# Chunk 4's decay factors on another queue, and two weight transfers made four

## The chip, the cores and the metric

The kernel runs on one core of a Trainium2 chip. A core has a matrix engine (TensorE, PE in the profile; its weight loads are the row PEld), a vector engine (VectorE, DVE), a scalar engine (ScalarE, ACT), a general engine (GpSimd, POOL) and an engine that here only issues transfers (SyncE, SP). They run their own instruction streams and wait for each other by semaphores. Transfers are issued from POOL, SP or ACT and carried by 16 DMA engines that all queues share. The metric is the device time of one execution in microseconds (us); lower is better.

## The reference

Two stages follow each other: a gated linear attention, and a bilinear feed-forward layer on its output.

```python
# q, k, v, alpha: (4, 8, 768, 48); alpha between 0.8 and 1.0
for t in range(S):
    state = alpha[:, :, t, :, None] * state + np.einsum('bhd,bhe->bhde', k[:, :, t], v[:, :, t])
    y[:, :, t] = np.einsum('bhd,bhde->bhe', q[:, :, t], state)
x = y.transpose(0, 2, 1, 3).reshape(3072, 384)
out = ((x @ w_a) * (x @ w_b)) @ w_out        # w_a, w_b: (384, 1536), w_out: (1536, 384)
```

## The kernel before

**Tiling.** The work is cut into six chunks. A chunk holds two of the four batches (chunks 0, 2, 4 the first two, 1, 3, 5 the other two) and 256 of the 768 time steps; time goes on from chunk 0 to 2 to 4. Inside a chunk the two batches are called pair 0 and pair 1 (`u`), and the 256 steps lie as 128 partitions by two neighbouring steps (`r`).

**One chunk of attention.** Its alphas are loaded (`ld a`), their logarithm is taken on ScalarE (`ln`, line 420), neighbouring steps are added (`l2`, `lx`), split in a rounded part and a rest (`H`, `L`, or `R` in later chunks) and summed over time on PE (`A2`, `AQ`). ScalarE makes the exponentials (`E`, line 541) and a ratio (`ra`, line 519). POOL or DVE corrects one of the two steps of q and k in place (`lv`, line 526; the k form reads the alphas again). DVE multiplies k and q with the exponentials into the tile QKp (`mk`, `mq`, line 552). QKp is turned so that the head dimension lies on the partitions: in chunks 0 and 1 by PE (`C`, line 593, copied by `Ce`), from chunk 2 on by a transposing transfer on SP (`T`, line 604). Then come the scores (`D`, line 674), their masking (`M`, or `Mc` on ScalarE and `Mm` on DVE), the state update (`K`, `KA`, `k`) and the outputs: `SB` opens the output banks and adds what one half carries into the other, `SA` adds what the carried state gives, `Y` adds the masked scores times v. `X` copies the result out of PSUM; from chunk 2 on it is turned by another transposing transfer on SP (`XT`, line 771).

**The feed-forward layer.** d_ff is cut into twelve blocks of 128 columns. `a f w` and `b f w` multiply block f of w_a or w_b with the chunk's y (line 786); w is `0` or `1` for one pair (256 columns, three matmuls) or `*` for both (512 columns). `as` copies the a product to SBUF on ScalarE (line 792), `pr` multiplies it with the b product on DVE (line 800). `o` multiplies by w_out (line 808), `ot` copies the result and `st` stores it on SP. The last number of a PE step is its PSUM bank, of eight; a step that takes a bank waits until the reader of what stood in it is through.

**Order.** The whole order is written out by hand in the string PROGRAM (lines 17 to 267), one step after the other, as `chunk: step arguments`. Each engine runs its own steps in this order; the letters V, P, S and Y at a step's end choose DVE, POOL, ScalarE or SP. A step that has to wait holds up whatever comes behind it on its engine. A transfer takes one of eight semaphores of its queue in turn, so an issue also waits until the eighth transfer before it on that queue has landed.

**What the change touches.** The weights w_a and w_b come on POOL's queue (`W w lo hi`, line 393), cast from float32 to bfloat16 on the way, in columns 0 to 256, 256 to 768 and 768 to 1536. A feed-forward block f uses columns 128 f to 128 f + 128, so columns 256 to 768 are the blocks 2 to 5. Chunk 0's feed-forward starts on lines 20 to 46 of PROGRAM with pair 0, while pair 1's attention is still under way, and chunk 1's attention is woven into it.

The tiles of the alphas (`a_t`) have two buffers, so chunk 4 takes chunk 2's, after chunk 2's `lv` of k. Chunk 4's alphas are issued on POOL's queue (line 98), between `lv 1 k P` and `lv 0 q P` of chunk 2. Chunk 5's are issued on SP's queue (line 142), just behind chunk 2's two turned outputs (`XT 1`, `XT 0`). The logarithm's tile has one buffer. A gate is one element copied on POOL, which makes POOL wait for what that element belongs to:

```python
def gate_m(x, u, h):
    nc.gpsimd.tensor_copy(go, x.m[int(u), int(h)][0:1, 0, 0, 0, 0:1])
```

Of the kernel before, what the change touches and what calls it, by code (L numbers as in the profile page):

```python
# [20 lines left out]
0: cm 1; ld v 1 P; c2 P; c3 P; D 0 1 5; M 0 1; D 0 0 0; SB 0 6; B 1a 4; Bs 1a; Mc 0 0; Mm 0 0 V; B 1b 5; Bs 1b; E 1a i; E 1a b; mq 1a V; mk 1a V; K 0 1 4; E 1b i  # L21
0: v 1 V; mk 1b V; E 1b b; mq 1b V; SA 0; Y 0; X 0 S; dk 1 0; C 1 0 3; Ce 1 0 V; k 0 1 V; b 1 0 6; W a 0 256; de 1; K 1 0 5; k 1 0 V
1: ld a 1 P
0: W a 256 768; W b 256 768
1: ld a 0 P
0: W a 768 1536; C 1 1 1; a 1 0 2; as 1 0; pr 1 0; Ce 1 1 V; W b 768 1536
1: ld q 0 P; ln 1
0: b 0 0 4; a 0 0 2; as 0 0; pr 0 0; D 1 0 6; D 1 1 0; M 1 1
1: ld k 0 P; l2 1 P; ld v 0 P; ld k 1 P
0: Mc 1 0; Mm 1 0 V  # L30
1: H 1 S
0: SB 1 1; a 2 0 3; a 5 0 6; a 3 0 7; as 3 0; a 4 0 4; as 4 0; as 5 0; b 4 0 0; b 3 0 7
1: L 1 V
0: pr 4 0; pr 3 0; SA 1; Y 1; X 1 V; b 2 0 0
1: A2 1 7; ld q 1 P
0: Wo 0 6
2: ld a * P
0: K 1 1 5
1: ln 0
0: as 2 0; pr 2 0  # L40
1: l2 0 V; E 1 b; E 1 i; H 0 S
0: a 3 1 4; a 5 1 2; k 1 1 V; as 3 1; b 3 1 0; a 4 1 1; b 5 0 7; pr 5 0; as 5 1; a 6 * 5; b 5 1 4; a 11 * 3; pr 5 1; pr 3 1; as 4 1; b 4 1 1; pr 4 1
1: L 0 V; dk * 6
0: Wo 6 12; as 11 *; as 6 *
1: ra 0
0: b 6 * 3; pr 6 *; b 11 * 0; pr 11 *
# [1 line left out]
1: lv 0 q P  # L48
2: ld q * P
1: ld v 1 P; lv 0 k V; mk 0 V  # L50
0: a 10 * 2; a 7 * 3
1: E 0 b; mq 0 V
0: as 10 *; a 2 1 4; as 2 1; b 10 * 1; pr 10 *; as 7 *; b 7 * 0; pr 7 *
1: v 0 S; ra 1
0: b 2 1 3; a 0 1 5
1: C 0 0 4
0: a 1 1 6; as 1 1
1: Ce 0 0 S
0: pr 2 1; b 1 1 1; pr 1 1; as 0 1
1: KA 0 02; k 0 0 V; k 0 1 V; C 0 1 7  # L60
0: b 0 1 6
1: Ce 0 1 S
2: ld k * P
1: lv 1 k P
0: pr 0 1
1: mk 1 V; lv 1 q P; mq 1 V
3: ld a * P
0: a 8 * 1; as 8 *; a 9 * 5; as 9 *
2: ld v * P
0: b 8 * 2; pr 8 *  # L70
1: D 0 0 6; M 0 0; D 0 1 3; Mc 0 1; SB 0 4
# [21 lines left out]
1: a 7 0 3; b 11 0 1; pr 11 0; KA 1 64; k 1 0 V; k 1 1 V; b 10 0 5; a 10 0 7; as 10 0; a 0 0 6  # L93
2: lv 0 k V
1: pr 10 0; b 0 0 1; a 3 0 4; as 0 0; pr 0 0
2: lv 1 k P; mk 1 V
1: as 3 0; b 3 0 7; a 1 0 6; as 1 0
4: ld a * P
1: b 7 0 0; b 1 0 4; pr 1 0; as 7 0; pr 7 0; pr 3 0
2: mk 0 V  # L100
1: SB 1 0
3: ln *
1: a 6 0 2; as 6 0; b 9 0 3; a 4 0 5; a 9 0 6; as 9 0; pr 9 0
2: mq 1 V; T 1
0: o 2 0 4
1: b 4 0 6; b 6 0 7
2: lv 0 q P; mq 0 V
1: pr 6 0
2: T 0
3: ld k * Y  # L110
# [24 lines left out]
2: D 0 0 5; Mc 0 0; Mm 0 0 V; gatem 0 0; SB 0 1; SA 1; Y 1; X 1 S; XT 1  # L135
3: lv 0 k P; lv 1 k P
1: a 4 1 7
4: ln *
1: as 4 1; b 9 1 0; pr 9 1; o 0 0 5
3: AQ 3  # L140
2: SA 0; Y 0; X 0 S; XT 0
5: ld a * Y
1: o 0 1 -; ot 0 V; a 1 1 6; a 10 1 1; as 1 1; as 10 1
3: E 0 b; E 0 i
1: b 4 1 2; pr 4 1; b 8 1 5; b 1 1 1; a 8 1 6; b 10 1 0; pr 1 1; o 3 0 2; pr 10 1; as 8 1; pr 8 1; o 3 1 -; ot 3 S; st 3 Y
# [3 lines left out]
3: E 1 i  # L149
1: st 0 Y  # L150
3: dr
4: lx V; R 0
3: mk 0 V; mq 0 V; T 0
4: ld q * Y
2: a 1 * 2; b 5 * 0; as 5 *; pr 5 *
4: ra 1
2: b 7 * 4; b 10 * 1; pr 4 *; a 10 * 6; as 10 *; pr 10 *
3: mk 1 V
2: a 7 * 0; b 1 * 5; a 0 * 6; b 0 * 7; as 1 *; as 7 *; pr 1 *; pr 7 *; as 0 *; a 3 * 0; b 9 * 1; pr 0 *
3: mq 1 V  # L160
# [5 lines left out]
3: KA * 06; D 0 0 4; M 0 0; dl; k * 0 V; k * 1 V  # L166
1: o 1 0 2
2: b 11 * 7
5: ln *
2: a 11 * 5; as 11 *; pr 11 *  # L170
1: o 1 1 -; ot 1 S
2: a 6 * 5; as 6 *; a 8 * 3; as 8 *
3: SB 0 6; D 0 1 0; M 0 1; T 1
4: ld k * Y
3: D 1 0 4; Mc 1 0
2: b 6 * 2; pr 6 *; b 8 * 3; pr 8 *
4: R 1
# [16 lines left out]
3: a 11 * 5  # L194
2: ot 2 V; ot 3 V
4: mq 0 V; mk 0 V
5: lx V
3: a 9 * 3; a 0 * 2; a 8 * 6; b 11 * 7; as 9 *; as 11 *; as 0 *; pr 11 *; b 9 * 2; b 0 * 1; pr 9 *
5: lv 0 k V
3: as 8 *  # L200
# [70 lines left out]
def kernel(  # L271
# [11 lines left out]
    nc = tc.nc  # L283
    B, H, S, D = q.shape
    assert (B, H, S, D) == (4, 8, 768, 48)
    C = 128
# [14 lines left out]
    ld = ctx.enter_context(tc.tile_pool(name="ld", bufs=2))  # L301
# [21 lines left out]
    go = cst.tile([1, 1], F32, name="go")  # L323
    S0 = [cst.tile([C, B, D + P2 * VS], BF16, name=f"S0{i}") for i in range(2)]
    Sm = [cst.tile([C, 2, D + P2 * VS], BF16, name=f"Sm{i}") for i in range(2)]
    QKp = [cst.tile([C, 2, 2, 2, H, DP], BF16, name=f"QKp{i}") for i in range(2)]
# [9 lines left out]
    def const_fill():  # L336
        nc.vector.memset(wz, 0.0)
        nc.vector.memset(og, 0.0)  # L338
        for g in range(2):
            nc.vector.memset(og[g * HC:(g + 1) * HC, g:g + 1], 1.0)  # L340
# [517 lines left out]
    def gate_m(x, u, h):  # L858

        nc.gpsimd.tensor_copy(go, x.m[int(u), int(h)][0:1, 0, 0, 0, 0:1])  # L860

    def gate_t(x, u):

        nc.gpsimd.tensor_copy(go, x.kqT[int(u)][0:1, 0, 0, 0, 0:1])

    OPS = {
        "gatet": gate_t,
        "gatem": gate_m,
        "c1": lambda x: const_fill(),
        "c1a": lambda x: const_table(),  # L870
# [99 lines left out]
```

## Time and profile before

| what | value |
|---|---|
| median of three runs | 194.94 us (194.47, 194.94, 197.66) |
| the profiled execution, its time | 193.93 us |
| its span, from first to last instruction | 192.2 us |
| granted TensorE clock | 0.999 |
| bytes moved by DMA | 30.96 MB, mean 161 GB/s |
| POOL's queue (software) | 18640 packets, 14.16 MB, 41.9% of 16 engines' span |
| SP's queue (hardware) | 48352 packets, 16.34 MB, 40.6% of 16 engines' span |
| instruction fetches | 19 packets, 0.31 MB |
| v of one batch in chunks 0 and 1 | 192 KB each, issued on POOL, one of them at 10.59 us |

Times in the profile count from the first instruction. A busy row gives an engine's busy time, its share of the span and its instructions. The row of DMA tenths cuts the span into 40 slices of 4.8 us; each digit is the busy share in tenths. A timeline row gives start, length, engine, line, operation, what is written from what is read, the count and, in square brackets, the idle time before it and what ended it. A group of matmuls ends later than its last issue, since matmuls are pipelined; what counts is when the next one starts. A row of the chain gives start, length and what worked. A row of a table by windows gives the stretch, its length and the busy time of PE, PEld, DVE, ACT and POOL with counts, the granted clock, the DMA engines' share and GB/s. A row of DMA issues gives what is written from what is read, the queue, how many, KB of each, and the time from issue to landing in us.

### The profile page before, as it was taken

To read this page: it belongs to the slowest core of one execution; us is meant where nothing else is said; L and a number is where in the kernel's file an instruction comes from. 1 tells how busy PE (TensorE), PEld (TensorE's weight loads), DVE (VectorE), ACT (ScalarE), POOL (GpSimd) and SP (SyncE) were. 2 spreads that over 40 slices of the span, in tenths; PEclk is the share of its full clock that TensorE was granted. 3 is DMA by queue.
4 is the path that set the end of the run, shared out by engine and by line. 5 is a ranking of instruction groups with operands and counts; after the bars stand their busy time and mean duration, and the time that the engine had idled before them with its cause. 6 is when DMAs were issued, how large, how long until landed. Compare 5 with 4: busy or idle time off the path is not lost.

```text
span 192.2 us, 5878 instructions
## 1 busy us (share of the span) xinstructions
PE 184.1 (96%) x2509; PEld 111.3 (58%) x2509; DVE 136.1 (71%) x230; ACT 103.1 (54%) x189; POOL 50.1 (26%) x72
## 2 busy tenths in 40 slices
PE   7979799999999998999999999999999999999993
PEld 3567576766777875644556644555544565544562
DVE  4778767999899796688979499864953961156520
ACT  4385566887585567446566135875266521164301
POOL 8999746920641404000400020050000000000000
PEclk9999999999999999999999999999999999999999
DMA  6999999999999999949993586998196005031013
GB/s 149 246 216 215 243 241 254 249 245 261 252 233 219 191 213 248 215 126 229 151 220 54 141 185 154 160 173 111 47 198 144 3 3 123 3 108 56 2 41 123
DMA packets 67162, 30.96 MB, mean 161 GB/s; under 512 B 58064, under 2 KB 65120, under 8 KB 67136
## 3 DMA queue, kind: packets, MB, share of 16 engines
q0 software_dynamic: 18640, 14.16, 41.9%
q1 hardware_dynamic: 48352, 16.34, 40.6%
q8 instruction: 19, 0.31, 0.7%
q10 hardware_dynamic: 144, 0.10, 0.2%
q14 instruction: 7, 0.06, 0.1%
HBM read 25.98 MB, written 4.74 MB: 160 GB/s over the span
## 4 chain that ended last, share of the span: by engine, by line
PE 86%; POOL 6%; DMA 4%; issue 1%; DVE 0%; ACT 0%; POOLq 0%; DVEq 0%
PE psum L786 48%; PE psum L808 24%; DMA wb_t<-in_moe_w_b_dram 4%; PE psum L674 3%; PE psum L724 2%; PE psum L627 2%; PE psum L698 2%; PE psum L703 1%; PE psum L507 1%; PE psum L819 1%; POOL v_t L413 1%; PE psum L593 1%; POOL a_t L413 1%; POOL wa_t L393 1%; POOL k_t L413 0%
## 5 line engine op out<-in xcount | busy, mean ns | idle before, releaser
L786 PE MATMUL psum<-xT,wb_t 128*128 128x512 bf16 (+1 forms) x270 | 57.0, 337 | 0.6 <-DMA wb_t<-in_moe_w_b_dram 0.5
L786 PE MATMUL psum<-xT,wa_t 128*128 128x512 bf16 (+1 forms) x270 | 56.1, 337 | 1.1 <-issue 0.7
L808 PE MATMUL psum<-wo_t,prod 128*128 128x384 bf16 x276 | 48.5, 326 | 0.0
L786 PEld LDWEIGHTS <-wb_t 128*128 128x128 bf16 x270 | 25.5, 98 | 21.1 <-DMA wb_t<-in_moe_w_b_dram 0.8
L786 PEld LDWEIGHTS <-wa_t 128*128 128x128 bf16 x270 | 25.6, 98 | 20.8 <-issue 1.0
L808 PEld LDWEIGHTS <-prod 128*128 128x128 bf16 x276 | 26.1, 98 | 16.9
L683 ACT ACTIVATE m<-psum 128x1024 bf16<-128x1024 f32 x16 | 16.3, 1023 | 6.5 <-PE psum L674 6.3
L825 DVE COPY ot<-psum 128x384 f32<-128x384 f32 (+1 forms) x13 | 6.9, 539 | 15.9 <-PE psum L808 13.4
L526 POOL TENSOR_TENSOR q_t<-q_t,ra 128x384 f32<-128x384 f32 x8 | 8.7, 1084 | 34.3 <-DMA q_t<-in_q_dram 17.3
L823 ACT ACTIVATE ot<-psum 128x384 f32<-128x384 f32 (+1 forms) x12 | 5.7, 477 | 12.9 <-PE psum L808 11.9
L420 ACT ACTIVATE la<-a_t 128x1536 f32<-128x1536 f32 (+2 forms) x9 | 9.5, 1057 | 3.4 <-DMA a_t<-in_alpha_dram 3.4
L687 DVE TENSOR_TENSOR m<-m,mask 128x1024 bf16<-128x1024 bf16 x16 | 10.8, 685 | 0.3 <-ACT m L683 0.3
L679 DVE TENSOR_TENSOR m<-psum,mask 128x1024 bf16<-128x1024 f32 x8 | 9.8, 1222 | 1.7 <-PE psum L674 1.5
L526 POOL TENSOR_TENSOR k_t<-k_t,a_t 128x384 f32<-128x384 f32 x5 | 5.3, 1064 | 19.0 <-DVE QKp L552 17.5
L552 DVE TENSOR_TENSOR QKp<-k_t,invb 128x768 bf16<-128x768 f32 x10 | 9.9, 992 | 0.2
L552 DVE TENSOR_TENSOR QKp<-q_t,beta 128x768 bf16<-128x768 f32 x10 | 9.3, 949 | 0.0
L674 PE MATMUL psum<-kqT 64*64 64x128 bf16 x384 | 8.6, 218 | 0.5 <-DVE prod L800 0.2
L413 POOL DMA_DIRECT2D v_t<-in_v_dram x8 | 8.6, 1070 | 0.5 <-issue 0.4
L674 PEld LDWEIGHTS <-kqT 64*64 64x64 bf16 x384 | 6.3, 107 | 3.2 <-issue 2.1
L764 ACT ACTIVATE ys<-psum 128x768 bf16<-128x768 f32 x7 | 5.6, 809 | 4.3 <-PE psum L703 2.3
L413 POOL DMA_DIRECT2D a_t<-in_alpha_dram x6 | 6.3, 1042 | 4.0 <-DMA wa_t<-in_moe_w_a_dram 2.2
L446 PE MATMUL psum<-wz 128*128 128x512 bf16 x17 | 5.5, 472 | 1.2 <-DVE og L338 1.2
(273 smaller groups left out, 270.9 us busy)
## 6 DMA issues: line engine op xcount, KB each, us to landing
out_dram<-ot SPq DMA_DIRECT2D x23, 192.0 KB, 2.2
a_t<-in_alpha_dram POOLq DMA_DIRECT2D x3, 768.0 KB, 14.5
k_t<-in_k_dram SPq DMA_DIRECT2D x3, 768.0 KB, 7.2
q_t<-in_q_dram POOLq DMA_DIRECT2D x2, 768.0 KB, 13.0
v_t<-in_v_dram POOLq DMA_DIRECT2D x4, 384.0 KB, 10.1
q_t<-in_q_dram SPq DMA_DIRECT2D x2, 768.0 KB, 6.6
a_t<-in_alpha_dram POOLq DMA_DIRECT2D x3, 384.0 KB, 5.6
q_t<-in_q_dram POOLq DMA_DIRECT2D x3, 384.0 KB, 13.4
```

The costliest lines, as they stand in the source:

```text
L413: eng.dma_start(out=t[:, us, hs].rearrange("p b h r d -> p (b h) (r d)"), in_=src[ch.b0 + us.start:ch.b0 + us.stop, hs, ch.s * 2 * C:(ch.s ...
L420: nc.scalar.activation(out=ch.la[:, us, hs].rearrange("p b h r d -> p (b h r d)"), in_=ch.a[:, us, hs].rearrange("p b h r d -> p (b h r d) ...
L526: eng.tensor_mul(x, x, by)
L552: eng.tensor_mul(QKp[ch.c % 2][:, u, j, :, hs, :D], src[:, u, hs].rearrange("p h r d -> p r h d"), f)
L674: nc.tensor.matmul(s2[g * HC:(g + 1) * HC, r, p, rk, :], lhsT=ch.kqT[u][rs, 1, rk, 2 * h + p, g * HC:(g + 1) * HC], rhs=queriesT(ch, u, 2 ...
L679: nc.vector.tensor_mul(m.rearrange("p r a k s -> p (r a) (k s)"), ch.s2[u, h].rearrange("p r a k s -> p (r a) (k s)"), maskn(4))
L683: nc.scalar.activation(out=m.rearrange("p r a k s -> p (r a) (k s)"), in_=ch.s2[u, h].rearrange("p r a k s -> p (r a) (k s)"), func=AF.Copy)
L687: eng.tensor_mul(x, x, maskn(4))
L786: nc.tensor.matmul(p, lhsT=(wa_t, wb_t)[w][:, kk, f * 128:(f + 1) * 128], rhs=ch.xT[:, us.start // 2:us.stop // 2, kk].rearrange("p u g s ...
L808: nc.tensor.matmul(op, lhsT=ch.prod[:, f, at:at + C], rhs=wo_t[:, f, :], start=(f == 0), stop=(f == NFF - 1))
L823: nc.scalar.activation(out=o_, in_=i_, func=AF.Copy)
L825: eng.tensor_copy(o_, i_)
```

## The change

Four things are done. The first is the weights' columns 256 to 768: two transfers of 512 columns become four of 256, in the order a, b, a, b. The second is chunk 0's order of blocks 2 to 5 and what lies around them: pair 1's `SB` goes ahead of the second scores, the blocks are taken in the order in which their columns come, `H` and `L` of chunk 1's pair 1 go behind them, and some banks are renumbered. A few steps further on change places (`a 10`, `b 5 1`, `b 4 1`, `pr 7`, and `a 1 1` ahead of chunk 1's first turn `C 0 0`). The third is chunk 4's alphas: they leave POOL's queue and take the place behind chunk 2's turned outputs on SP, where chunk 5's were; chunk 5's go behind chunk 4's k; the logarithms and sums of both move down accordingly. The fourth is chunk 2's products: `mq 1` and the turn `T 1` come ahead of `mk 0`, and a new gate on POOL holds `lv 0 q` until `mk 1` is through.

```diff
-0: W a 256 768; W b 256 768
+0: W a 256 512; W b 256 512; W a 512 768; W b 512 768
 1: ld a 0 P
...
-0: b 0 0 4; a 0 0 2; as 0 0; pr 0 0; D 1 0 6; D 1 1 0; M 1 1
+0: b 0 0 4; a 0 0 2; as 0 0; pr 0 0; D 1 0 6; SB 1 2; D 1 1 0; M 1 1
 1: ld k 0 P; l2 1 P; ld v 0 P; ld k 1 P
 0: Mc 1 0; Mm 1 0 V
-1: H 1 S
-0: SB 1 1; a 2 0 3; a 5 0 6; a 3 0 7; as 3 0; a 4 0 4; as 4 0; as 5 0; b 4 0 0; b 3 0 7
-1: L 1 V
-0: pr 4 0; pr 3 0; SA 1; Y 1; X 1 V; b 2 0 0
+0: a 2 0 4; as 2 0; a 3 0 5; as 3 0; b 2 0 6; pr 2 0; b 3 0 0; a 4 0 7; as 4 0; a 5 0 1; as 5 0; pr 3 0
+1: H 1 S; L 1 V
+0: SA 1; Y 1; X 1 V; b 4 0 4; pr 4 0; b 5 0 5; pr 5 0
 1: A2 1 7; ld q 1 P
...
-0: K 1 1 5
+0: K 1 1 6
 1: ln 0
-0: as 2 0; pr 2 0
 1: l2 0 V; E 1 b; E 1 i; H 0 S
-0: a 3 1 4; a 5 1 2; k 1 1 V; as 3 1; b 3 1 0; a 4 1 1; b 5 0 7; pr 5 0; as 5 1; a 6 * 5; b 5 1 4; a 11 * 3; pr 5 1; pr 3 1; as 4 1; b 4 1 1; pr 4 1
-1: L 0 V; dk * 6
+0: a 3 1 1; a 5 1 2; k 1 1 V; as 3 1; b 3 1 0; a 4 1 3; as 5 1; b 5 1 4; as 4 1; b 4 1 5; pr 3 1; pr 5 1; a 6 * 6; a 11 * 7; pr 4 1
+1: L 0 V; dk * 1
+0: a 10 * 2
...
-0: a 10 * 2; a 7 * 3
+0: a 7 * 4
...
-0: b 2 1 3; a 0 1 5
-1: C 0 0 4
-0: a 1 1 6; as 1 1
+0: b 2 1 3; a 0 1 6; a 1 1 4
+1: C 0 0 5
+0: as 1 1
...
-2: lv 1 k P; mk 1 V
+2: lv 1 k P; mk 1 V; gatek 1; lv 0 q P
 1: as 3 0; b 3 0 7; a 1 0 6; as 1 0
-4: ld a * P
 1: b 7 0 0; b 1 0 4; pr 1 0; as 7 0; pr 7 0; pr 3 0
-2: mk 0 V
+2: mq 1 V; T 1
...
-2: mq 1 V; T 1
+2: mk 0 V
 0: o 2 0 4
 1: b 4 0 6; b 6 0 7
-2: lv 0 q P; mq 0 V
+2: mq 0 V
...
-4: ln *
...
 2: SA 0; Y 0; X 0 S; XT 0
-5: ld a * Y
+4: ld a * Y
...
-4: lx V; R 0
 3: mk 0 V; mq 0 V; T 0
 4: ld q * Y
 2: a 1 * 2; b 5 * 0; as 5 *; pr 5 *
-4: ra 1
-2: b 7 * 4; b 10 * 1; pr 4 *; a 10 * 6; as 10 *; pr 10 *
+4: ln *; ra 1
+2: b 7 * 4; b 10 * 1; pr 4 *
+4: lx V
+2: a 10 * 6; as 10 *; pr 10 *
...
-5: ln *
...
 2: a 6 * 5; as 6 *; a 8 * 3; as 8 *
+4: R 0
 3: SB 0 6; D 0 1 0; M 0 1; T 1
 4: ld k * Y
+5: ld a * Y
...
-5: lx V
+5: ln *; lx V
...
+    def gate_k(x, u):
+
+        nc.gpsimd.tensor_copy(go, QKp[x.c % 2][0:1, int(u), 1, 0, 0, 0:1])
```

More of the change, by code (lines that the diff above doesn't have):

```diff
@@ L50 @@
 1: ld v 1 P; lv 0 k V; mk 0 V
-0: a 10 * 2; a 7 * 3
+0: a 7 * 4
 1: E 0 b; mq 0 V
-0: as 10 *; a 2 1 4; as 2 1; b 10 * 1; pr 10 *; as 7 *; b 7 * 0; pr 7 *
+0: as 10 *; a 2 1 5; as 2 1; b 10 * 1; as 7 *; b 7 * 0; pr 7 *; pr 10 *
 1: v 0 S; ra 1
-0: b 2 1 3; a 0 1 5
-1: C 0 0 4
-0: a 1 1 6; as 1 1
+0: b 2 1 3; a 0 1 6; a 1 1 4
+1: C 0 0 5
+0: as 1 1
 1: Ce 0 0 S
-0: pr 2 1; b 1 1 1; pr 1 1; as 0 1
-1: KA 0 02; k 0 0 V; k 0 1 V; C 0 1 7
-0: b 0 1 6
+0: pr 2 1; b 1 1 7; pr 1 1; as 0 1
+1: KA 0 02; k 0 0 V; k 0 1 V; C 0 1 1
+0: b 0 1 4
 1: Ce 0 1 S
@@ L67 @@
 3: ld a * P
-0: a 8 * 1; as 8 *; a 9 * 5; as 9 *
+0: a 8 * 7; as 8 *; a 9 * 5; as 9 *
 2: ld v * P
@@ L867 @@
         "gatet": gate_t,
+        "gatek": gate_k,
         "gatem": gate_m,
```

## The prediction

> **What bounds the kernel now.** I read the page first: busy times, DMA slices, queues.
>
> ```profile
> PE 184.1 (96%) x2509; PEld 111.3 (58%) x2509; DVE 136.1 (71%) x230; ACT 103.1 (54%) x189; POOL 50.1 (26%) x72
> DMA  6999999999999999949993586998196005031013
> ```
>
> PE is 96% busy, and the DMA engines are full from the second slice to about 80 us (16 slices of 4.8 us). Busy PE need not be fast PE, so I looked at the chain and then at busy time by stage.
>
> ```profile
> 81.25 11.65 PE psum L786 x54
> ...
> 12.80:24.40 11.60, 9.56 (x245) 7.43 (x244) 9.70 (x20) 7.07 (x16) 10.40 (x13) 1.00 1.26 219
> 24.40:65.10 40.70, 40.70 (x575) 29.14 (x574) 35.53 (x66) 28.80 (x61) 17.75 (x17) 1.00 1.23 238
> ...
> 75.90:77.10 1.20, 0.48 (x5) 0.26 (x3) 0.56 (x1) 0.00 (x0) 0.45 (x1) 1.00 1.69 102
> 77.10:189.00 111.90, 111.88 (x1263) 60.50 (x1262) 73.81 (x111) 52.07 (x89) 6.25 (x6) 1.00 0.59 114
> ```
>
> The chain's 54 matmuls of 512 columns take 216 ns each, 2.4 columns per ns at a granted clock of 1.00: back to back. The windows' first two numbers are length and PE busy time. PE is idle 2.04 us between 12.8 and 24.4, 0.72 at 76 and 0.02 after 77; a last 0.22 at 66 stands in the timeline below. The change adds and removes no matmul and touches nothing before 12.8, so all it can win is these 3.0 us, 1.5% of the time; nothing after 77 can be won, only lost. The PE timeline shows the places.
>
> ```profile
> 19.95 0.33 PE L698 MATMUL psum<-kqT,Sm 64*64 64x128 bf16 x6
> 20.67 1.48 PE L786 MATMUL psum<-xT,wa_t 128*128 128x256 bf16 x12 [0.39 <-DMA wa_t<-in_moe_w_a_dram]
> 22.65 0.83 PE L786 MATMUL psum<-xT,wb_t 128*128 128x256 bf16 x6 [0.50 <-DMA wb_t<-in_moe_w_b_dram]
> ...
> 25.51 0.83 PE L786 MATMUL psum<-xT,wa_t 128*128 128x256 bf16 x6
> ...
> 35.26 0.61 PE L593 MATMUL psum<-ident,QKp 128*128 128x128 bf16 x8
> ...
> 66.12 0.64 PE L674 MATMUL psum<-kqT 64*64 64x128 bf16 x32 [0.22 <-DVE prod L800]
> ...
> 77.04 0.60 PE L786 MATMUL psum<-xT,wa_t 128*128 128x256 bf16 x4 [0.72 <-issue]
> ```
>
> **Part 1: four weight transfers for two.** POOL's issue and the transfers' landing:
>
> ```profile
> 8.38 0.77 POOL L393 DMA_DIRECT2D wb_t<-in_moe_w_b_dram  x1
> 12.02 0.76 POOL L393 DMA_DIRECT2D wa_t<-in_moe_w_a_dram  x1
> 13.69 0.75 POOL L393 DMA_DIRECT2D wa_t<-in_moe_w_a_dram  x1
> 14.42 0.76 POOL L393 DMA_DIRECT2D wb_t<-in_moe_w_b_dram  x1
> ```
> ```profile
> wa_t<-in_moe_w_a_dram POOLq DMA_DIRECT2D x1, 576.0 KB, 10.4
> wb_t<-in_moe_w_b_dram POOLq DMA_DIRECT2D x1, 576.0 KB, 12.7
> ...
> wa_t<-in_moe_w_a_dram POOLq DMA_DIRECT2D x1, 384.0 KB, 6.9
> wb_t<-in_moe_w_b_dram POOLq DMA_DIRECT2D x1, 384.0 KB, 8.2
> wb_t<-in_moe_w_b_dram POOLq DMA_DIRECT2D x1, 192.0 KB, 6.1
> wa_t<-in_moe_w_a_dram POOLq DMA_DIRECT2D x1, 192.0 KB, 4.6
> ```
>
> Two more issues of 0.75 us put everything behind them on POOL 1.5 us later: chunk 1's a, q, k and v loads, the last weight columns, and the l2 addition. The cover is the queue: the last weight columns land 10.4 and 12.7 us after their issue because the transfers ahead are not through. Without that cover it costs up to 1.5 us.
>
> Landing, issue plus landing time: the 384 KB pair at 13.69 + 6.9 = 20.6 and 14.42 + 8.2 = 22.6, so about 2 us per 384 KB. The earlier 192 KB ones land at 14.5 and 16.6 with another 192 KB (chunk 0's v) between them, which is 1.05 us each: the same rate. So splitting costs nothing by that row. The other end: if a packet cost the same however short, one sees the price in the window in which the 384 KB pair moves.
>
> ```profile
> q0 software_dynamic: 730, 1.01, 116.7%
> ```
>
> That is 1.167 x 16 x 4.3 us / 730 = 110 ns a packet (window 18.3 to 22.6). Each pair is 768 row packets; twice as many add 768 x 110 / 16 = 5.3 us. The range is 0 to 5.3 us, and a gain is excluded since no byte goes. I take 0.2, by the 192 KB row, which is the same packet form. [...]
>
> **Part 2: chunk 0's order.** The new landings are then about 19.7, 20.7, 21.7 and 22.8. PE is through with the earlier scores and carried products at 20.28 (19.95 + 0.33). It finds a 2 and a 3 loaded, then b 2 and b 3, then a 4 and a 5: six groups of 0.33, to about 22.5, then SA and Y. Both stalls, 0.39 and 0.50, go. What is late next is ScalarE: H now stands behind as 5, so H, then L on DVE, then the evacuation X, end near 25.0. a 3 1 starts at 25.05 instead of 25.51, and b 5 0 (0.33) is already done: 0.8 us ahead. The group needing the last wb columns stays at 29.5 (16.79 + 12.7 in the trace of before) plus 0.2.
>
> Most of that lead is taken back at 35.26, chunk 1's first turn on PE. It needs the q product:
>
> ```profile
> 32.61 0.56 DVE L526 TENSOR_TENSOR k_t<-k_t,a_t 128x384 f32<-128x384 f32 x1 [0.31 <-DMA k_t<-in_k_dram]
> ...
> 34.15 0.95 DVE L552 TENSOR_TENSOR QKp<-q_t,beta 128x768 bf16<-128x768 f32 x1
> ```
>
> DVE waited for k's landing at 32.6 and finishes q at 35.10; that does not move with PE. The new order puts a 1 1 (0.33 us) ahead of this turn, so what is kept is 0.16 + 0.33 = 0.49, less the 0.2 of part 1, plus something for the k half of the turn, which can start before q. Bounds -0.3 (all of 0.8 us delay) to 0.9; I take **0.4**.
>
> **Part 3: POOL loses chunk 4's alphas; q of pair 1 and its turn go first.**
>
> ```profile
> 54.70 1.19 POOL L413 DMA_DIRECT2D a_t<-in_alpha_dram  x1 [1.89 <-DVE prod L800]
> ...
> 56.41 1.36 DVE L552 TENSOR_TENSOR QKp<-k_t,invb 128x768 bf16<-128x768 f32 x1
> ...
> 59.03 7.19 SPq L604 DMA_TRANSPOSE kqT<-QKp  x2
> ```
> ```profile
> L604 SPq DMA_TRANSPOSE kqT<-QKp x8: 1732/2066/4955, 59.0 to 140.3; - x8
> ...
>   PEld L674: 0.5, 1
> ```
>
> The scores at 66.12 belong to the first turn (59.03). The PE row names a DVE product, but a weight load waited 0.5 us for the turn itself. That turn held SP for 4.96 us against a median of 2.07, while chunk 4's 768 KB were in the queues. Afterwards mq 1 takes the place of mk 0 at 56.4, so the turn is issued 1.2 to 1.6 us sooner, and the 768 KB are gone from 55 to 63. The wait of 0.22 (PE row) to 0.5 us goes: **0.4**, and the lead from part 2 survives. The gate (one element on POOL, waiting for mk 1) holds only lv 0 q behind it, which waited for DVE there before too: nothing.
>
> **Part 4: alphas through SP.** Chunk 4's 768 KB take the slot of chunk 5's, which slide behind chunk 4's k.
>
> ```profile
> a_t<-in_alpha_dram POOLq DMA_DIRECT2D x3, 768.0 KB, 14.5
> k_t<-in_k_dram SPq DMA_DIRECT2D x3, 768.0 KB, 7.2
> ...
> a_t<-in_alpha_dram SPq DMA_DIRECT2D x1, 768.0 KB, 6.4
> ```
> ```profile
> 77.30 0.45 SPq L413 DMA_DIRECT2D a_t<-in_alpha_dram  x1
> ...
> 83.64 0.55 ACT L519 ACTIVATE ra<-la 128x384 f32<-128x384 f32 x1
> 86.46 0.60 ACT L792 ACTIVATE as__1828<-psum 128x512 bf16<-128x512 f32 x1 [2.27 <-PE psum L786]
> ...
> 87.56 0.81 PE L786 MATMUL psum<-xT,wa_t 128*128 128x512 bf16 x3
> ...
> 92.79 1.48 ACT L420 ACTIVATE la<-a_t 128x1536 f32<-128x1536 f32 x1
> ```
>
> Issue at 77.30 plus 6.4 is 83.7. ScalarE now has chunk 4's logarithm (1.48, as chunk 5's at 92.79) just ahead of the 86.46 row, with the ratio (0.55) behind it, so 83.7 + 2.0 = 85.7 is in time by 0.8 us. Queued behind the wait are as 10 (86.46) and every later copy of chunk 2, and on DVE lx, which needs the logarithm, and the products behind it. PE takes as 10's bank again with a 0 (87.56), 0.5 us after as 10 ends at 87.06, so the cover is 0.8 + 0.5 = 1.3 us, and beyond it the price is one for one. Chunk 5's alphas go out behind chunk 4's k, and their logarithm moves from 92.79 to twelve ScalarE steps later, behind chunk 4's exponentials; no row here dates that place, and a late landing would show as a wait of la. Cost 0.
>
> **Part 5: the 0.72 us at 77.** PE stops inside a group of three with nothing awaited. I read it as an instruction fetch behind busy DMA engines. With 768 KB less before it, it may shrink; bounds 0 to 0.72, I take half, **0.35**. [...]
>
> **Sum.** 0.4 + 0.4 + 0.35 = 1.15 us off the profiled run's 193.93 (its span is 192.2, 1.7 lies around it): 192.8. The median of the three runs is 194.94, 1.0 above that execution, so I forecast 193.8 for a median.
>
> **Rivals.**
> (A) Data stays the limit: the lead is lost at 35.26, the turn at 66 waits for another transfer, the fetch stays. For it: full DMA slices to 80 us. Against: 768 KB leave that stretch. Time 194.9, within 0.4.
> (B) Slower: short packets cost as much as long ones. Place: b 6, the first group on the last wb columns, which PE reaches about 4.7 us after 25.05 (six groups of 0.33, three of 0.65, and some 0.8 of decay products, an estimate), at 29.7. The columns land at 29.5 + 5.3 = 34.8, a stall of 5.1, less the lead of 0.8 and the 0.75 of parts 3 and 5: +3.55, 198.5. Half the price gives 195.8, and it decides from 0.2 + 0.8 + 0.75 = 1.75 us on. The 192 KB landings speak against it.
> (C) Slower: chunk 4's alphas take the 14.5 us that POOL's 768 KB took, not 6.4. Landing at 91.8 is 6.8 us past the 85.0 that the cover allows; less the gains of 1.15, +5.65, 200.6. Against: both SP rows, 6.4 and 7.2.
>
> **Chances.** Forecast 0.60, A 0.22, B 0.10, C 0.08. The likeliest case's own range is the best sum, 0.9 + 0.5 + 0.72 = 2.1 off 194.47, so 192.4, to 194.7. Runs of before scatter from 194.47 to 197.66. Taking in A, the cheaper half of B and the scatter, the range is 192.0 to 197.0. About 2% is what a measurement of this kernel can tell from no change (191.0 and 198.8). Faster than that needs more than PE's idle time, so only scatter gives it: 0.06. Slower by that: a part of B near its full price, most of C and some scatter, 0.12. Within: 0.82.
>
> **What would show it.** Part 1: four wa and wb landings, the last near 22.8. Part 2: no DMA releaser on PE before 25, and the a 3 1 row near 25.0; a wait at the turn near 35. Part 3: a turn issued near 57.5 and held on SP for about 2 us, and no idle before the scores at 65. Part 4: PE solid after 77; a wait of ScalarE's la on alphas above 2 us near 83 means C. Part 5: the row with issue as releaser. A DMA wait on wb_t near 30 would prove me wrong through B.

## The result, and the profile after

| kernel | median | lowest to highest | executions |
|---|---|---|---|
| before | 194.69 us | 193.96 to 197.66 | 22 |
| changed | 195.73 us | 194.53 to 197.78 | 22 |

The changed kernel takes 1.0051 times as long, with a 95% interval of 1.0031 to 1.0072: about 1 us slower. The time lies within the range of the prediction, but a gain was forecast. In 13 of the changed kernel's 34 executions (these 22 and 12 in a later run) the mean granted clock was below 0.995; "at the full clock" below means without such executions, which gives a median of 195.58 us here. The profiled execution had the full clock, took 195.06 us and has a span of 193.3 us, against 193.93 and 192.2 before.

The page's busy and DMA rows first, as they were read of before:

```profile
PE 185.2 (96%) x2509; PEld 112.4 (58%) x2509; DVE 134.5 (70%) x230; ACT 103.6 (54%) x189; POOL 49.8 (26%) x74
...
DMA  5999999999999895979999397999297005021013
```

The engines are as busy as before. Twelve of the 40 DMA digits differ, most of them by one or two. The widest difference is slice 22 (about 101 to 106 us), which has a 9 now and had a 3 before: a stretch in which the DMA engines had been mostly free is now full, and that is where the microsecond was lost. The windows of the prediction say more (length, busy time of PE, PEld, DVE, ACT and POOL, granted clock, DMA share, GB/s):

```profile
12.80:24.40 11.60, 10.37 (x248) 8.27 (x246) 9.32 (x20) 7.60 (x17) 11.55 (x15) 1.00 1.31 209
24.40:65.10 40.70, 40.70 (x578) 29.08 (x573) 35.28 (x66) 28.81 (x61) 16.93 (x18) 1.00 1.25 235
65.10:66.10 1.00, 1.00 (x21) 0.73 (x22) 0.75 (x2) 0.71 (x3) 0.49 (x1) 1.00 0.79 158
...
75.90:77.10 1.20, 1.20 (x12) 1.03 (x11) 0.56 (x1) 0.55 (x3) 0.33 (x1) 1.00 0.05 14
77.10:189.00 111.90, 110.08 (x1245) 58.90 (x1244) 73.04 (x110) 53.09 (x89) 5.63 (x6) 1.00 0.64 120
```

PE is busier up to 24.4 us (10.37 instead of 9.56), and the idle times at 66 and 77 us are gone. In exchange PE stands idle for 111.90 - 110.08 = 1.82 us after 77, where it had been idle for 0.02. PE's waits and its timeline name the place:

```profile
PE psum L723 <- issue: 1.8, 1, 1.8
PE psum L445 <- DVE og L337: 1.2, 1, 1.2
PE psum L626 <- ACT prod L540: 0.6, 1, 0.6
PE psum L592 <- DVE QKp L551: 0.5, 1, 0.5
PE psum L785 <- DVE m L678: 0.2, 1, 0.2
```
```profile
65.94 0.64 PE L673 MATMUL psum<-kqT 64*64 64x128 bf16 x32
...
76.03 0.82 PE L785 MATMUL psum<-xT,wa_t 128*128 128x256 bf16 x6
76.68 1.17 PE L785 MATMUL psum<-xT,wb_t 128*128 128x256 bf16 x9
...
103.55 0.45 PE L723 MATMUL psum<-v_t,m 64*128 64x48 bf16 x22
105.82 0.30 PE L723 MATMUL psum<-v_t,m 64*128 64x48 bf16 x10 [1.82 <-issue]
```

(Line numbers are one lower than before, since PROGRAM has one line less.) The DMA waits on weights have left the list, and one line leads it that was not there: 1.8 us in line 723, the product of a masked score tile with v. It breaks off after 22 of its 32 small matmuls, with nothing awaited. That is the form of the 0.72 us at 77 us before: a stop inside a group, put down to issue.

**What "issue" is here.** If PE's instructions, weight loads and matmuls, are counted from the start in order of time, the stop at 77 us before comes at instruction 2493 and the one at 104 us at 3262: 769 apart, three times 256 and one. The trace has a queue of its own for instructions, with 19 packets and 0.31 MB, so 16 KB each. Both stops lie at instruction 445 + 256 n, within one (n is 8 and 11), and so do those that the experiments below number (2238, 2494, 3261, 3262). In the dense stretches a packet begins soon after PE has passed instruction 240 + 256 n (0.2 to 0.4 us for block 11 before and for blocks 16 and 17 in both kernels); I take that number, an estimate from the packets that came soonest, as the point at which block n is asked for, 205 instructions ahead of the one at which PE runs dry. (Elsewhere some came earlier: blocks 9, 12, 15 and 18 moved when PE was 11 to 69 instructions short of that number, in both kernels.) The DMA view of two stretches of the changed kernel shows when block 11 came; PE passed its number, 3056, at 100.05 us.

```profile
DMA packets 2458, 0.81 MB, mean 257 GB/s; under 512 B 2458, under 2 KB 2458, under 8 KB 2458
## 3 DMA queue, kind: packets, MB, share of 16 engines
q1 hardware_dynamic: 1778, 0.68, 88.5%
q0 software_dynamic: 680, 0.13, 47.2%
```
```profile
q1 hardware_dynamic: 752, 0.22, 231.0%
q8 instruction: 1, 0.02, 5.8%
```

The first rows are 100.1 to 103.25 us, the others 103.25 to 104.55 us (the share adds up the times of all packets, so it can pass 100%). For 3.2 us SP's and POOL's queues fill the engines and no instruction packet moves; then it comes, from 103.30 to 104.51 us, and PE goes on at 105.8. Before, the same block was asked for at 100.84 and moved 0.3 us later, at 101.14 to 102.16, while PE was still busy; the queues in 101.1 to 102.2 us before were nearly empty:

```profile
q0 software_dynamic: 64, 0.01, 13.0%
q8 instruction: 1, 0.02, 5.8%
```

What had changed is SP's queue:

```profile
92.97 1.09 SPq L412 DMA_DIRECT2D k_t<-in_k_dram  x1
94.17 2.49 SPq L412 DMA_DIRECT2D a_t<-in_alpha_dram  x1
```

Chunk 5's alphas are issued behind chunk 4's k at 94.17, beside chunk 4's v on POOL (93.14). These three transfers land at 105.76, 100.48 and 103.63 us by their records. Before, k and v alone were in the queues there, through at 101.0 and 102.7.

### The profile page after: what moved, and what is told of

Its sections match the earlier page's. It is cut to its first block, busy times and chain, and to the rows that moved or that the text cites. A ratio compares the mean times of both kernels' runs of the same rounds, so it can differ in the third digit from the quotient of the medians.

```text
span 193.3 us, 5884 instructions
## 1 busy us (share of the span) xinstructions
PE 185.2 (96%) x2509; PEld 112.4 (58%) x2509; DVE 134.5 (70%) x230; ACT 103.6 (54%) x189; POOL 49.8 (26%) x74
## 4 chain that ended last, share of the span: by engine, by line
PE 86%; POOL 4%; DMA 3%; DVE 2%; issue 2%; ACT 0%; POOLq 0%
PE psum L785 48%; PE psum L807 24%; DMA v_t<-in_v_dram 3%; PE psum L673 3%; PE psum L723 2%; PE psum L697 2%; PE psum L626 2%; PE psum L702 1%; PE psum L506 1%; PE psum L818 1%; PE psum L592 1%; DVE m L678 1%; DVE kqT L600 1%; POOL mask L365 1%; POOL v_t L412 1%
## 5 line engine op out<-in xcount | busy, mean ns | idle before, releaser
L525 POOL TENSOR_TENSOR q_t<-q_t,ra 128x384 f32<-128x384 f32 x8 | 8.1, 1014 | 33.5 <-ACT as__1878 L791 16.0
L540 ACT ACTIVATE invb<-psum 128x384 f32<-128x384 f32 x10 | 4.9, 502 | 3.2 <-PE psum L511 1.7
```

Source lines behind the costliest of these rows:

```text
L525: eng.tensor_mul(x, x, by)
```

## The experiments

"Alphas" are always the 768 KB of one chunk. The lead in the table below is the time at which PE starts its n-th instruction, less that time in the profile of before (the second column); it is worked out from the traces' PE records, and a minus sign is earlier than before. At instruction 430, ahead of the change's first effect, these executions differ by up to 1.59 us (first row). At 800 the order of the work differs between the two starts, so the n-th instruction is not the same work there; from 1000 on it is.

| PE instruction | before, us | changed | start only | alphas only | v later | alphas twice | next to each other |
|---|---|---|---|---|---|---|---|
| 430 | 16.41 | 0.72 | 0.35 | 0.79 | 0.95 | 0.49 | 1.59 |
| 800 | 27.92 | -0.22 | -0.94 | 0.95 | -0.18 | 0.39 | 0.31 |
| 1000 | 36.60 | 0.11 | 0.07 | 0.95 | 0.15 | 0.46 | 0.63 |
| 1880 | 66.13 | -0.18 | 0.06 | 0.67 | 0.02 | 0.54 | 0.35 |
| 2500 | 77.36 | -0.79 | 0.04 | 0.16 | -0.59 | 0.49 | -0.06 |
| 3250 | 104.54 | -0.79 | 0.04 | 0.16 | -0.58 | 0.48 | 0.89 |
| 3270 | 104.67 | 1.19 | 0.04 | 2.17 | 0.56 | 2.14 | 1.24 |
| 5000 | 187.99 | 1.19 | 0.03 | 2.17 | 0.66 | 2.27 | 1.24 |

**Next to each other: chunk 5's alphas right behind chunk 4's**

```diff
 4: ld a * Y
+5: ld a * Y
...
 4: ld k * Y
-5: ld a * Y
```

> The changed kernel with one step moved: chunk 5's alphas are issued right behind chunk 4's (near 78 us) and not behind chunk 4's k (near 94). Theory F (the changed kernel's loss is PE running out of instructions at 103.8 us, because chunk 5's alphas share the DMA engines with the instruction fetch there): the 1.82 us before the matmuls of line 723 goes, the span comes to 191.0 to 192.0, and the time is 0.9 to 1.8 us under the changed kernel's 195.73, so a ratio to before of 0.995 to 1.000. Rival G (the loss is in chunk 0's new order or in the four weight transfers, and the stall is an accident of one execution): the ratio stays at 1.005.

Measured: 195.01 us against 194.78 (ratio 0.9996, 0.9965 to 1.0028), at the full clock 194.88; span 193.3. Of PE's waits and its timeline in this run, with one row of DVE and one of SP:

```profile
PE psum L702 <- DVE prod L799: 0.9, 1, 0.9
...
PE psum L702 <- issue: 0.3, 1, 0.3
...
PE psum L723 <- issue: 0.2, 1, 0.2
```
```profile
99.23 0.18 PE L702 MATMUL psum<-Sm,kqT 64*64 64x48 bf16 x1 [0.88 <-DVE prod L799]
```
```profile
96.80 0.56 DVE L662 TENSOR_TENSOR Sm<-tmp,bl 128x384 bf16<-128x384 f32 x1 [1.31 <-DMA bl<-row]
```
```profile
81.74 2.57 SPq L840 DMA_DIRECT2D out_dram<-ot  x2
```

The 1.8 us shrank to 0.2, so it goes with the alphas' place, as expected. But 0.9 us came up elsewhere. Behind two alpha loads in a row SP's next issues are late (the stores of 81.74 take 2.57 us, 0.82 in the changed kernel), so the decay rows `bl` reach DVE late, and PE waits for what DVE then does late: the state and a product behind it. One wait was exchanged for another.

**Alphas twice: the kernel before, with one more load in the suspected place**

```diff
 4: ld k * Y
+5: ld a * Y
```

> The kernel before with one transfer more: chunk 5's alphas are loaded a second time, behind chunk 4's k (near 94 us), 768 KB that nothing needs so early. Theory F: an idle of 1 to 2 us whose releaser is issue stands on PE near 103 and the ratio to before is 1.004 to 1.010. Rival G: PE has no idle there, since the scores, sums and outputs of that stretch need no byte of this transfer, and the ratio is within 0.2% of 1.

Chunk 5's alphas are loaded a second time here, over the same values. Measured: 196.24 us, ratio 1.008 (1.0049 to 1.0112).

```profile
PE psum L725 <- issue: 1.5, 1, 1.5
...
PE psum L787 <- issue: 0.7, 1, 0.7
```

Nothing else of the change is in this kernel, and the idle time is there: 1.5 us at 105.1 us, instruction 3261, block 11 moving 2.75 us after it was asked for. The old 0.7 us at 77 stays as well. This is the plainest of the runs: 768 KB more in that place cost the kernel before some 1.5 us.

**Start only**, the kernel before with the four weight transfers and chunk 0's order, and **alphas only**, the rest of the change without them:

```diff
-0: W a 256 768; W b 256 768
+0: W a 256 512; W b 256 512; W a 512 768; W b 512 768
...
-0: a 10 * 2; a 7 * 3
+0: a 7 * 4
```

> The kernel before with parts 1 and 2 of the change alone: the four weight transfers and chunk 0's new order; the alphas of chunks 4 and 5 and chunk 2's products as before. Theory F: the two stalls on the weights go, what is kept is 0.2 to 0.6 us, and the idle at 77 us stays; ratio 0.997 to 1.000. Rival G: the loss is here, ratio 1.004 to 1.008.

The alphas only, against the kernel before:

```diff
-2: lv 1 k P; mk 1 V
+2: lv 1 k P; mk 1 V; gatek 1; lv 0 q P
...
-4: ld a * P
...
-2: mk 0 V
+2: mq 1 V; T 1
...
-5: ld a * Y
+4: ld a * Y
...
+5: ld a * Y
```

> The kernel before with parts 3 and 4 of the change alone: chunk 4's alphas on SyncE's queue, chunk 5's behind chunk 4's k, the gate and the earlier turn; weights and chunk 0's order as before. Theory F: the wait before the scores at 66 us and the idle at 77 us go (0.4 to 1.1 us), and an idle of 1 to 2 us with releaser issue comes near 103; ratio 1.002 to 1.008. Rival G: the ratio is 0.994 to 0.998, since only gains are in this half.

Measured: start only 194.34 us, ratio 0.9982 (0.9957 to 1.0007); alphas only 197.34 us, ratio 1.0129 (1.0077 to 1.018). At the full clock alphas only takes 196.02 us (two of six executions), 1.2 us over the 194.78 of the kernel before, so about half of its 2.6 us goes with the clock. In the start-only run's PE timeline no row has a DMA as releaser before the turn at 35 us:

```profile
20.34 0.82 PE L785 MATMUL psum<-xT,wa_t 128*128 128x256 bf16 x6
20.99 0.49 PE L785 MATMUL psum<-xT,wb_t 128*128 128x256 bf16 x3
21.72 0.49 PE L785 MATMUL psum<-xT,wb_t 128*128 128x256 bf16 x3 [0.24 <-DVE m L678]
...
25.22 0.83 PE L785 MATMUL psum<-xT,wa_t 128*128 128x256 bf16 x6
...
35.25 0.39 PE L592 MATMUL psum<-ident,QKp 128*128 128x128 bf16 x4
35.87 0.40 PE L592 MATMUL psum<-ident,QKp 128*128 128x128 bf16 x4 [0.23 <-DVE QKp L551]
```

PE has a 1 1 done when it comes to the turn at 35.25 us, a lead of some 0.3 us, and gives it back there: the second half of the turn waits for QKp, and at 36.6 us PE is 0.07 us later than before (table). The stop at 77 us stays, at instruction 2494, with block 8 moving 3.1 us after it was asked for; its row names a ScalarE copy as the releaser (0.69 us). The alphas-only run has the idle times of the changed kernel's second half: none at 66 and 77, and this at instruction 3261:

```profile
106.79 0.31 PE L724 MATMUL psum<-v_t,m 64*128 64x48 bf16 x11 [1.84 <-issue]
```

So the stop at 104 us, and the loss, belong to the alphas' part of the change, and the start, taken alone, loses nothing.

**v later: chunk 4's v behind the state of chunk 3, with chunk 5's alphas as changed**

```diff
-4: lv 0 q P; ld v * P
+4: lv 0 q P
...
+3: gatem 1 1
+4: ld v * P
```

> The changed kernel with chunk 4's v issued by POOL only after chunk 3's last masking (near 104 us, by a gate), not near 93: 384 KB less beside chunk 4's k and chunk 5's alphas. Theory F (the instruction fetch that PE needs by 103.8 us is late because the DMA engines are full from 93 to 106): the idle with releaser issue near 104 falls from 1.8 to under 0.5 us, nothing else moves, and the ratio to before is 0.993 to 0.999. Rival H (it is SyncE's queue that is late, by one more transfer in its order, and the idle is a consequence): the idle stays at 1 to 2 us and the ratio at 1.005.

Measured: 194.68 us against 194.92, ratio 0.9988 (0.9966 to 1.0011). With v out of the way the alphas land at 103.25 instead of 105.76 us, block 11 moves 2.2 instead of 3.25 us after it was asked for, and the idle time is about half:

```profile
105.18 0.30 PE L725 MATMUL psum<-v_t,m 64*128 64x48 bf16 x10 [0.97 <-issue]
```

I had expected under 0.5. The direction holds: the same load in the same place, fewer bytes beside it, a shorter stop.

**More instructions: 96 more PE instructions at the start, the same columns**

```diff
-fill 7 2
+warm 28 2
...
-fill 9 2
+warm 36 2
```

> The changed kernel with its 16 filling matmuls of 512 columns at the start made 64 of 128 columns: the same columns, 96 more instructions on PE ahead of everything else. Theory F, in its sharpest form (PE reads its instructions in blocks of 256 and stops at a block's end): an idle with releaser issue again stands 205 instructions after the 12th block's request, which is now 96 instructions earlier in the program, in the matmuls of line 807 or 506 at 102 to 103 us and not in those of line 723; its length may be 0.5 to 2 us. Rival H (the idle belongs to what those matmuls of line 723 need): it stays in line 723.

Warming matmuls of 512 columns, whose product nobody reads, become four of 128 each. Measured: 195.53 us, ratio 1.0016 (0.9983 to 1.005).

```profile
103.19 0.36 PE L506 MATMUL psum<-l,utb 64*64 64x384 bf16 x2
104.33 0.36 PE L506 MATMUL psum<-l,utb 64*64 64x384 bf16 x2 [0.78 <-issue]
```
```profile
69.96 0.35 PE L673 MATMUL psum<-kqT 64*64 64x128 bf16 x9 [0.71 <-issue]
```

The stop is at instruction 3262 again, and since 96 instructions were put ahead, that is now another line, 506, earlier in the program. A second stop appears at 69.0 us, instruction 2238 = 445 + 7 x 256 + 1. Here neither the place in the program nor the operands matter; the number does.

**Chunk 5's alphas behind chunk 4's q, and v later**

```diff
 4: ld q * Y
+5: ld a * Y
...
 4: ld k * Y
-5: ld a * Y
```

(The edit of "v later" is in this kernel as well.)

> The changed kernel with chunk 5's alphas behind chunk 4's q (near 86 us) and chunk 4's v later as well. Theory F: no idle with releaser issue near 104; the alphas now stand ahead of chunk 3's decay rows on SyncE's queue, whose landing held DVE for 1.3 us where the alphas stood still earlier, so up to 1 us may be lost near 98; ratio 0.994 to 1.002. Rival H: issue idle near 104 stays, ratio 1.005 or more.

Measured: 196.75 us, ratio 1.0093 (1.0067 to 1.0119); I had expected 0.994 to 1.002. The last alpha rows are in at 95.06 us, and no wait has issue as its releaser, but two others come up:

```profile
98.93 0.18 PE L704 MATMUL psum<-Sm,kqT 64*64 64x48 bf16 x1 [1.39 <-DVE prod L801]
...
112.93 1.24 PE L787 MATMUL psum<-xT,wa_t 128*128 128x512 bf16 x5 [1.47 <-DVE QKp L553]
```

The early place clears PE's code and delays the state again, as when the loads stood next to each other. The second row names a DVE product, but this matmul does not read QKp. It reads chunk 3's turned output `xT`, whose transfer landed at 112.80 us, 0.1 us before it started (110.00 in the changed kernel). That transfer was under way beside v, which was issued at 105.53 and landed at 113.04. Two earlier places on SP were tried, near 79 and near 86 us, and each brought a wait of its own.

**The changed kernel again**, unaltered:

> The changed kernel itself once more, beside the others on the same chip. Both theories: ratio 1.003 to 1.008. Theory F: an idle of 1 to 2 us with releaser issue in line 723 near 104 in this execution too, and none at 77.

Measured: 196.89 us, ratio 1.007 (1.0035 to 1.0105). The stop repeats:

```profile
107.92 0.30 PE L723 MATMUL psum<-v_t,m 64*128 64x48 bf16 x10 [2.03 <-issue]
```

At the full clock the median is 195.03 us (five of 12 executions) against 194.92, 0.1 us more, where the first series has 0.9 us (195.58 against 194.69). So the stop repeats, but how much time it costs in the end is less sure than the first median makes it look.

**224 more instructions, on the start only and on the changed kernel**

```diff
-fill 7 2
+fill 2 2; warm 82 2
...
-fill 9 2
+fill 4 2; warm 40 2
...
-            nc.tensor.matmul(bank(i)[:, :C], lhsT=wz[:, :C], rhs=wz[:, :C], start=True, stop=True)
+            nc.tensor.matmul(bank(i)[:64, :48], lhsT=wz[:64, :64], rhs=wz[:64, :48], start=True, stop=True)
```

> The kernel before with the changed kernel's start, as in the run with the start only, and 224 more instructions in the warming matmuls ahead of PE's 50th instruction (sixteen 512-column matmuls become six, and 122 small ones of 64 x 48 are added; their product is read by nobody). Theory (PE's code comes in blocks of 256 instructions, block n is asked for at about instruction 240 + 256 n and PE stands still from 445 + 256 n if it has not come): in the run with the start only, the block of the idle time at 77 us was asked for at 71.6 us and was late; now the same block boundary falls 224 instructions of the program earlier, so the dry points are those that had the numbers 2013, 2269 and 2525 there, which were started at 67, 71.5 and 79 us, and the blocks for them are asked for at 62, 67.5 and 72 us, 4 to 7 us ahead. The idle time at 77 us (0.7 us) goes and none over 0.5 us takes its place; span 191.2 to 191.8, time 0.6 us less than the run with the start only, 193.5 to 194.0, if the start is no later. Rival (idle time there is a full queue's, whatever the instruction number): 0.7 us stays at 77 us and the time is that of the run with the start only, 194.3, or more by what the small matmuls delay in the start.

> The changed kernel with the same 224 instructions more ahead of PE's 50th; chunk 5's alphas and the other loads as in the changed kernel. Theory of the instruction blocks: the block that came too late at 104 us was asked for at 100 us (instruction 3056); now the boundaries fall at the places which had the numbers 2832 (asked, near 94 us) with 3037 (dry, near 100 us) and 3088 (asked, 100.3 us) with 3293 (dry, near 106 us). With a fetch of 3.3 us and 1 us each for its transfer and for PE to go on, the idle time of 1.8 us at 104 us falls to under 0.8 us in all between 90 and 110 us, with chunk 5's alphas where they were; span 191.7 to 192.6, time 1 us less than the changed kernel's, 194.2 to 195.0. Rival (chunk 5's alphas delay the values or the keys of chunk 4, and PE would wait there anyway): PE waits 1.5 us or more between 97 and 112 us, by another name than issue, and the time is the changed kernel's, 195.7.

Measured: start only with 224 more 198.18 us, ratio 1.0166 (1.0131 to 1.0202). This was a poor design: the 82 small matmuls ran 4.57 us, 56 ns each, and the start came 3 us later. The stop did not go, either:

```profile
2.17 4.57 PE L449 MATMUL psum<-wz 64*64 64x48 bf16 x82
...
76.23 0.57 PE L723 MATMUL psum<-v_t,m 64*128 64x48 bf16 x31 [0.70 <-issue]
```

It is again at instruction 2494, as in the run with the start only, now a place in line 723 that the program reached at 75.3 us, and block 8 moved 2.7 us after it was asked for. The number held; my forecast that the block would be early enough there was wrong. The changed kernel with 224 more instructions gave no reading: its profiled execution took 1052 us, while the five others took 197.55 to 202.14. In it a 512-column matmul of line 785 took 1694 ns on average (379 ns in the changed kernel), from start to end, with a clock recorded as 1.00. I don't know why, and nothing is concluded from it.

**Fewer instructions, on the start only and on the changed kernel**

```diff
-fill 7 2
+warm 3 2
...
-fill 9 2
+warm 4 2
...
+            nc.tensor.matmul(bank(i)[:, :256], lhsT=wz.bitcast(F32)[:, :C], rhs=wz.bitcast(F32), start=True, stop=True)
```

> The kernel before with the changed kernel's start, as in the run with the start only, and 18 PE instructions fewer at the very start: the sixteen warming matmuls of 512 columns (their product is read by nobody) become seven of 256 columns in float32, which take about as long together less 0.4 to 0.9 us; each matmul is two instructions. Theory (PE stands still at instruction 445 + 256 n if block n has not come): instruction 2493, where the run with the start only stood idle from 76.2 to 77.2 us, is now a place 18 instructions later in the program, some 9 matmuls of 512 columns or 2 us further on, at about 78 us, and the block is there by 77. The idle time of 0.7 us goes; span 191.2 to 191.8, time 193.5 to 194.0. Rival (the idle time belongs to the place or to the full queue): 0.7 us stays near 77 us and the time is 194.3.

> The changed kernel with the same 18 PE instructions fewer at the very start, chunk 5's alphas and all loads as in the changed kernel. Theory of the instruction blocks: instruction 3262, where the changed kernel stood idle from 103.8 to 105.8 us in line 723, is now a place 18 instructions later, in the output product behind it (line 807), which is reached near 104.6 us, while the block comes at the same time. The idle time stays at instruction 3262, is now in line 807, and is 0.8 to 1.2 us instead of 1.8; span 192.2 to 192.8, time 194.8 to 195.2. Rival (PE waits for chunk 5's or chunk 4's data at line 723): 1.8 us stays in line 723 and the time is 195.7.

Measured: start only 194.16 us, ratio 0.9959 (0.9935 to 0.9984); changed 196.48 us, ratio 1.0084 (1.0052 to 1.0115), at the full clock 195.44 (five of nine executions) against 194.88. The edit was smaller than I wrote: the trace shows two matmuls for each float32 one.

```profile
1.20 2.93 PE L449 MATMUL psum<-wz 128*128 128x256 f32 x6 [1.20 <-DVE og L337]
```

Three became six in that row, and the other four became eight, so sixteen matmuls became fourteen: four instructions fewer, not 18. With that, the two stops are as the theory has them, two matmuls further on in the program than they were:

```profile
103.80 0.47 PE L723 MATMUL psum<-v_t,m 64*128 64x48 bf16 x24
106.07 0.27 PE L723 MATMUL psum<-v_t,m 64*128 64x48 bf16 x8 [1.80 <-issue]
```

Line 723 now breaks off after 24 matmuls instead of 22, at instruction 3262. In the start-only version line 785 breaks off after five instead of three, at 2494, for 0.58 us. That version is the fastest of all and faster than both kernels. What the warming edit adds to the start alone is not settled: the two intervals overlap, and the idle time is nearly the same.

## Why the prediction was wrong

**The step that failed is part 4, "Cost 0".** I checked chunk 4's alphas against their deadline and was right: issued at 77.88, landed at 83.27, 5.4 us instead of the 14.5 of rival C, and ScalarE waited 0.3 us for them. For chunk 5's alphas I looked only for who reads them ("a late landing would show as a wait of la"). I did not ask what else is carried by the DMA engines between 94 and 106 us. PE's own code is. The move set 768 KB beside k and v just when a dense stretch of small matmuls eats the 205 instructions from 3056 to 3262 in 3.8 us, and the code came 3.25 us after it was asked for instead of 0.3. That cost 2.0 us of lead (the table, -0.79 to 1.19), the largest single term of the whole change. The row of DMA tenths that the prediction shows has a 3 in slice 22: the engines were mostly free where the code came, and the move filled them.

**Part 5 had the cause and missed its use.** Reading the 0.72 us at 77 us as an instruction fetch behind busy engines was right; I took half of it, 0.35, and it went whole: PE runs through 77 us, and from the instruction at 66.13 us to the one at 77.36 its lead grows by 0.61 us (-0.18 to -0.79). The same sentence, applied to the stretch into which the bytes were moved, would have given the loss. (Of the changed kernel's 19 packets of code, 16 KB each, one stands behind a wait in the list of PE's waits, and that one cost 1.8 us.)

**Part 3 held.** The turn is issued at 57.69 instead of 59.03, holds SP for 3.1 us instead of 4.96 (I had said about 2), and its scores start without idle time; the lead grows by 0.29 us there, and by 0.28 in the alphas-only run, where I had 0.4.

**Part 1 held.** The four transfers landed at 19.69, 20.81, 21.77 and 23.22 us, the last 4.26 us behind chunk 1's alphas ahead of them; before, the second landed 4.38 us behind. The split costs nothing, and rival B is false: no DMA wait on wb_t near 30 us.

**Part 2 held in its mechanism.** Both weight waits went. The a 3 1 row starts at 25.94 instead of 25.51; this execution was 0.72 us late at instruction 430, so the row comes 0.29 us sooner, and b 5 0 (0.33) is done by then: about 0.6 us, predicted 0.8. Counted from instruction 430, 0.61 us of lead are left at 36.6 us in the changed kernel (0.72 to 0.11) and 0.28 in the start-only run (0.35 to 0.07), where I took 0.4. How much the change keeps there cannot be read from one execution, since the data's arrival at the turn does not follow PE's start; the times of the start-only run give between 0.1 us lost and 0.8 us won (its interval, of 194.78 us). A wait of 0.24 us for the mask product at 22.4, from a renumbered bank, was not foreseen.

**The sum.** Predicted: 0.4 + 0.4 + 0.35 won. Shown: 0.3 at the turn, 0.6 net at 77 us, some tenths or nothing from the start, and 2.0 lost at 104 us: a loss of 0.5 us between the two profiles, counted from instruction 430 (0.72 to 1.19), and of about 1 us if nothing is kept from the start; the medians have 1.0, and at the full clock 0.9 and 0.1. Of the named cases rival A (194.9) came nearest in time, but its mechanism did not occur: the early waits did go. Half of rival B's price gives 195.8, and that is luck, since no weight columns came late. That the time lies within the range is luck too: no case in it has the stop at 104 us.

**What stays open.** Why the lower granted clock came more often with the alphas' part of the change (13 of 34 executions of the changed kernel and 4 of 6 of alphas only, against 9 of 89 of the kernel before and none of 12 of start only) is not shown. That full DMA engines delay the code is shown by the runs that add, move or remove transfers (block 11 moved 0.3 us after its number before, 3.25 in the changed kernel, 2.75 with the alphas twice, 2.2 with v later); when a block is really asked for is an estimate.

## What to carry to other kernels

A transfer that is moved has two kinds of neighbours: those who read it, and whatever shares the DMA engines at its new time, the engines' own code among it. Look for idle time with issue as releaser inside a group; if such places are multiples of 256 instructions apart, as here (769, within one), dense small matmuls may be running into late code blocks, and a large load just before such a stretch is the first suspect (768 KB cost 1.8 us of idle time here). To find whether an idle time belongs to a place or to an instruction number, put a few instructions ahead of it and see which of the two it keeps.

## What the runs showed of the hardware

In dense stretches PE asked for a block of 256 instructions about 205 ahead of need, by the estimate above. Block 11 moved 0.3 us later at 101 us before, with nearly empty queues and no stop. At the stops the block moved 3.3 us later (77 us before), 3.25 (the changed kernel), 3.1 (start only), 2.75 (alphas twice), 2.7 (224 more on the start only) and 2.2 (v later). PE also ran through blocks that moved up to 2.7 us late (block 14 of the changed kernel), where the 205 instructions took longer (6.9 us there, against 3.8 at the stop). After the stop it went on 1.2 us behind the packet's end before (75.82 to 77.04 us) and 1.3 us in the changed kernel (104.51 to 105.82). A stop stayed at one number, within one, while its place in the program moved by 4 (2494 and 3262), 96 (3262) or 224 instructions (2494).

In the second profile of the changed kernel the clock was at half for 6.8 us early in the execution (windows 10.88 to 17.71 us and the stretch behind it):

```profile
10.88:17.71 6.83, 6.68 (x124) 5.67 (x124) 4.46 (x9) 3.95 (x8) 6.78 (x11) 0.50 1.31 211
17.71:24.00 6.29, 5.98 (x132) 4.67 (x124) 5.25 (x11) 4.14 (x9) 5.19 (x7) 1.00 1.29 220
```

In the run with the alphas next to each other the mean clock of the first 26 us was 0.93, where it was 1.00 in both kernels' first profiles. No run here shows what sets it off.
